# Scores of all twelve tiles from plain fp32 q and k, each product in a quarter of TensorE's array

## The chip, the core and the metric

The kernel runs on one core of a Trainium2 chip. The metric is device time in microseconds for one execution of the whole program. Below, PE is TensorE's matmul side and PEld its weight loads, DVE is VectorE, ACT ScalarE, POOL GpSimd and SP SyncE, which mostly issues DMAs.

## The reference

A gated linear attention (an mLSTM with a stabilised exponential gate) over 2 batches, 8 heads, 768 steps and a head size of 40; its output goes through a mixture of four dense experts and then through a gated product layer.

```python
for t in range(S):
    kt, vt, qt = (k[:, :, t], v[:, :, t], q[:, :, t])
    m_new = np.maximum(f_gate[:, :, t] + m, i_gate[:, :, t])
    ...
    C = f_stab[...] * C + i_stab[...] * np.einsum('bhd,bhe->bhde', vt, kt)
    n = f_stab[:, :, None] * n + i_stab[:, :, None] * kt
    h_tilde = np.einsum('bhde,bhe->bhd', C, qt)
    denom = np.maximum(np.abs(np.einsum('bhd,bhd->bh', n, qt)[:, :, None]), 1.0)
    y[:, :, t] = sigmoid(o_gate[:, :, t]) * h_tilde / denom
...
for e in range(E):                      # four experts, F = 1024, D = 320
    out += p[:, e:e + 1] * (np.maximum(x @ w1[e], 0.0) @ w2[e])
...
return ((x @ w_a) * (x @ w_b)) @ w_out  # d_ff = 1536
```

All inputs and the output are fp32.

## The kernel before

The 768 steps of each batch are cut into six chunks of 128, which gives twelve tiles; tile n is chunk n // 2 of batch n % 2. Within a tile the recurrence is solved in parallel form: the scores q k^T of each head (a 128 by 128 matrix, keys down the partitions) are multiplied by a matrix of gate weights and applied to v, and what older chunks contribute comes from a running state. A tile passes through these helpers, each one a few instructions:

- `load_qk` (L329) brings q and k, transposed, head dimension on the partitions, four heads side by side, once for each half hh of the heads;
- `w_exp` (L504 on ACT) and `w_mask` (L508 on POOL) make the gate weights `w_t`;
- the scores land in two PSUM banks `pt_c`, one for each half, and `s1b` (L530 on DVE) multiplies them into `w_t`;
- `s2a` (L541) applies them to v (`pt_y`, fp32, two column halves of the array side by side) and reads the state (`pt_i`, L547); `s2b`, `s2x` (L564) and `s2c` normalise, gate and pad the result `x_t`;
- `s3a` transposes it on PE (`pt_x`, L154 to L156), and `x_hi`, `x_lo` split it into two fp32r parts `xh`, `xl`, the input of the experts;
- `weigh_k`, `state` (`pt_u`, L604), `state_in`, `state_old`, `state_add` carry the state on.

The scores are made in two ways. Tiles 0 to 3 (n < NP = 4) use `scores2` (L510 to L518): q and k stay fp32, the two halves of the heads lie at partitions 0 and 64, and a product takes 40 rows of one half of the array's rows and all 128 columns; the heads are taken from the two halves in turn. Tiles 4 to 11 use `scores` (L520 to L526): q and k are loaded three times over into 120 rows, ACT casts all of it to fp32r (`split_qk`, L351), DVE or POOL replace one of three row groups of each operand by the rounding error (`low_qk`, L357), and one fp32r product over 120 rows then gives the score of a head in one pass.

Beside the tiles, from 17 us on, PE runs the first expert's products (`psa` L210, `psy` L289 to L291) as a stream of items; ACT and DVE evict each item (`hh` L277, `hl` L278), and ACT, POOL and DVE split the weights that come in (`wh` L78, `wl` L102). The place of every helper in this stream is written out by hand in the table `ev` (L711 to L809): pairs of a time, counted in items, and a helper; an engine's queue holds the instructions in that order. PSUM tiles of the helpers come from one pool of four banks (`ps_t`). At 151 us the tiles are through; the other experts and the last layer follow, in which PE is fed from SBUF alone.

Of the kernel before, what the change touches and what calls it, by code (L numbers as in the profile page):

```python
# [7 lines left out]
F32 = mybir.dt.float32  # L8
# [25 lines left out]
NP = 4  # L34
# [4 lines left out]
QB = 3  # L39
# [12 lines left out]
def mlstm_moe_kernel(ctx, tc, gates, qk, qc, kvo, dp, w1b, w2b, ident_d, bdmask_d, rsel_d, exp_d, out):  # L52
# [256 lines left out]
    with ExitStack() as c1:  # L309
# [19 lines left out]
        def load_qk(n, hh, eng=None):  # L329

            t = td.setdefault(n, {})
            if n < NP:
                if "two" not in t:
                    tag, bufs = ("qs", 2) if n == NP - 1 else ("qk", QB)
                    t["two"] = qp.tile([KS, 2, 512], F32, tag=tag, name="qk_t", bufs=bufs)
                at, r, to = 64 * hh, RQ, t["two"]
            else:
                to = t["qk", hh] = qp.tile([KS, 2, 512], F32, tag="qk", name="qk_t", bufs=QB)
                at, r = 0, KS
            v = to.rearrange("p a b -> p (a b)")  # L340
# [169 lines left out]
        def scores2(n):  # L510
# [3 lines left out]
            for h in range(4):  # L514
                hs = slice(h * P, (h + 1) * P)
                for hh in range(2):
                    v = t["two"][64 * hh:64 * hh + D]
                    nc.tensor.matmul(t["pc", hh][:, hs], v[:, 1, hs], v[:, 0, hs], start=True, stop=True, skip_group_check=True)  # L518

        def scores(n, hh, pool=ps_t, tag="t"):  # L520
            t = td[n]
            qs = t["qs", hh]
            t["pc", hh] = pc = pool.tile([P, 512], F32, tag=tag, name="pt_c")
            for h in range(4):
                hs = slice(h * P, (h + 1) * P)
                nc.tensor.matmul(pc[:, hs], qs[:, 1, hs], qs[:, 0, hs], start=True, stop=True, skip_group_check=True)  # L526
# [550 lines left out]
```

## Time and profile before

| | us |
|---|---|
| median of 3 runs | 597.9 (596.6 to 600.08) |
| the profiled execution | 597.87 |
| its span, first to last instruction | 596.1 |
| PE busy | 586.3, 98% of the span |
| PEld busy | 555.6, 93% |
| DVE busy | 395.2, 66% |
| ACT busy | 268.2, 45% |
| POOL busy | 190.5, 32% |

The profiled execution lies 0.03 us below the median. The 1.8 us between its time and its span lie around the program and are not touched by any instruction. A busy PE is one that has a matmul in flight, not one at its peak: matmuls are pipelined, a record lasts longer than the step to the next one, so what a product costs is read from the start of one to the start of the next.

### The profile page before, as it was taken

To read this page: it belongs to the slowest core of one execution; us is meant where nothing else is said; L and a number is where in the kernel's file an instruction comes from. 1 tells how busy PE (TensorE), PEld (TensorE's weight loads), DVE (VectorE), ACT (ScalarE), POOL (GpSimd) and SP (SyncE) were. 2 spreads that over 40 slices of the span, in tenths; PEclk is the share of its full clock that TensorE was granted. 3 is DMA by queue.
4 is the path that set the end of the run, shared out by engine and by line. 5 is a ranking of instruction groups with operands and counts; after the bars stand their busy time and mean duration, and the time that the engine had idled before them with its cause. 6 is when DMAs were issued, how large, how long until landed. Compare 5 with 4: busy or idle time off the path is not lost.

```text
span 596.1 us, 14965 instructions
## 1 busy us (share of the span) xinstructions
PE 586.3 (98%) x6108; PEld 555.6 (93%) x6108; DVE 395.2 (66%) x813; ACT 268.2 (45%) x606; POOL 190.5 (32%) x246
## 2 busy tenths in 40 slices
PE   8999999999999999999999999999999999999997
PEld 5798999999899999999999999999898989898887
DVE  6888877876423665645466666688688787875444
ACT  7879478683232444433233332334455534341211
POOL 3966665650010333544022231221323222311000
PEclk9999999999999999999999999999999999999999
DMA  8979648750211333332111211515312121200012
GB/s 238 272 227 241 177 135 231 186 154 1 60 40 54 80 86 107 92 89 52 36 40 38 57 40 39 143 53 153 115 42 73 39 58 52 63 21 2 1 38 97
DMA packets 34626, 55.48 MB, mean 93 GB/s; under 512 B 3861, under 2 KB 22461, under 8 KB 34557
## 3 DMA queue, kind: packets, MB, share of 16 engines
q10 hardware_dynamic: 18992, 27.07, 16.4%
q1 hardware_dynamic: 14893, 25.48, 15.9%
q0 software_dynamic: 672, 1.97, 1.2%
q8 instruction: 48, 0.79, 0.6%
q14 instruction: 21, 0.17, 0.1%
HBM read 50.15 MB, written 3.96 MB: 91 GB/s over the span
## 4 chain that ended last, share of the span: by engine, by line
PE 81%; DVE 7%; DMA 6%; ACT 2%; ACTq 2%; issue 2%; SPq 0%; DVEq 0%
PE psa L230 28%; PE psy L255 26%; PE psb L230 8%; PE psa L210 6%; DMA gt<-in_gates 3%; PE pt_y L541 2%; PE psy L289 2%; PE psy L291 2%; PE psy L290 2%; DMA qk_t<-in_qk 2%; PE pt_i L547 1%; PE pt_c L526 1%; PE pt_u L604 1%; DVE acc L300 1%; DVE g L914 1%
## 5 line engine op out<-in xcount | busy, mean ns | idle before, releaser
L255 PE MATMUL psy<-wh,hh 64*128 64x320 f32 x848 | 179.0, 306 | 1.5 <-ACT acc L890 1.5
L255 PE MATMUL psy<-wl,hh 64*128 64x320 f32 x848 | 178.7, 306 | 0.0
L255 PE MATMUL psy<-wh,hl 64*128 64x320 f32 x848 | 178.7, 306 | 0.0
L230 PE MATMUL psa<-xh,wh 64*128 64x512 f32 x648 | 147.5, 388 | 0.2 <-DVE g L914 0.2
L255 PEld LDWEIGHTS psy<-wh,hh 64*128 64x128 f32 x848 | 131.5, 184 | 2.6 <-ACT acc L890 1.9
L255 PEld LDWEIGHTS psy<-wh,hl 64*128 64x128 f32 x848 | 131.6, 184 | 0.0
L255 PEld LDWEIGHTS psy<-wl,hh 64*128 64x128 f32 x848 | 131.4, 184 | 0.0
L230 PE MATMUL psa<-xh,wl 64*128 64x512 f32 x468 | 109.4, 387 | 0.0
L230 PEld LDWEIGHTS psa<-xh,wh 64*128 64x128 f32 x648 | 92.9, 184 | 3.9 <-DVE g L914 0.8
L230 PE MATMUL psa<-xl,wh 64*128 64x512 f32 x432 | 95.3, 387 | 0.0
L911 DVE SCALAR_TENSOR_TENSOR hl<-psa,hh 128x512 fp32r<-128x512 f32 x72 | 46.3, 685 | 72.4 <-ACT hh L910 72.4
L134 POOL TENSOR_TENSOR wl<-tp,lf 128x272 fp32r<-128x272 f32 x48 | 39.1, 814 | 122.3 <-DVE tp L133 111.4
L230 PEld LDWEIGHTS psa<-xh,wl 64*128 64x128 f32 x468 | 69.6, 184 | 2.7
L230 PE MATMUL psb<-xh,wh 64*128 64x512 f32 x216 | 69.7, 388 | 0.0
L131 POOL TENSOR_TENSOR lf<-lf,sq 128x272 f32<-128x272 f32 x48 | 38.1, 795 | 95.4 <-ACT wh L130 72.2
L910 ACT ACTIVATE hh<-psa 128x512 fp32r<-128x512 f32 x72 | 39.1, 596 | 64.1 <-PE psy L255 33.4
L230 PEld LDWEIGHTS psa<-xl,wh 64*128 64x128 f32 x432 | 62.9, 184 | 2.5
L230 PE MATMUL psb<-xh,wl 64*128 64x512 f32 x180 | 58.2, 387 | 0.0
L130 ACT CAST wh<-tp 128x272 fp32r<-128x272 f32 x48 | 20.2, 420 | 68.7 <-DVE tp L127 66.4
L102 POOL TENSOR_TENSOR wl<-raw,wh 128x352 fp32r<-128x352 f32 (+1 forms) x30 | 28.4, 950 | 70.0 <-ACT wh L78 70.0
L230 PE MATMUL psb<-xl,wh 64*128 64x512 f32 x144 | 44.2, 387 | 0.0
L914 DVE TENSOR_TENSOR g<-psa,bs 128x512 f32<-128x512 f32 x36 | 24.7, 685 | 28.1 <-ACT bs L913 27.9
(147 smaller groups left out, 1254.5 us busy)
## 6 DMA issues: line engine op xcount, KB each, us to landing
raw<-in_w2b ACTq DMA_DIRECT2D x48, 272.0 KB, 2.8
qk_t<-in_qk SPq DMA_DIRECT2D x16, 480.0 KB, 6.2
raw<-in_w1b ACTq DMA_DIRECT2D x40, 176.0 KB, 2.3
acc<-in_w1b SPq DMA_DIRECT2D x22, 176.0 KB, 4.8
kvo_t<-in_kvo SPq DMA_DIRECT2D x10, 364.5 KB, 6.2
og_t<-in_kvo SPq DMA_DIRECT2D x6, 320.0 KB, 4.9
dz_t<-z_t ACTq DMA_DIRECT2D x12, 160.0 KB, 2.7
qc_t<-in_qc SPq DMA_DIRECT2D x10, 180.0 KB, 4.3
```

Of the source, the lines that this page charges most:

```text
L102: lo_eng.tensor_tensor(wl[:, ps], raw[:, k * st // parts:(k + 1) * st // parts], wh[:, ps].bitcast(F32), op=ALU.subtract)
L130: nc.scalar.copy(wh[:, cs], tf)
L131: nc.gpsimd.tensor_tensor(lf, lf, sq, op=ALU.mult)
L134: nc.gpsimd.tensor_tensor(wl[:, cs], tf, lf, op=ALU.add)
L210: nc.tensor.matmul(ps, l, r, start=(i == 0), stop=(i == len(prs) - 1))
L230: return nc.tensor.matmul(ps[g], w[rows, o:o + P], x, start=start, stop=stop)
L255: ms = [nc.tensor.matmul(ps[t], l[rows, t * P:(t + 1) * P], w[rows, off:off + DM], start=start, stop=stop) for t, rows in zip(two, (UP, DN))]
L289: nc.tensor.matmul(ps, lh, wh[:, off:off + DM], start=(fi == 0), stop=False)
L290: nc.tensor.matmul(ps, lh, wl[:, off:off + DM], start=False, stop=False)
L910: nc.scalar.activation(hh, ps[f], AF.Relu)
L911: nc.vector.scalar_tensor_tensor(hl, ps[f], 0.0, hh.bitcast(F32), op0=ALU.max, op1=ALU.subtract)
L914: nc.vector.tensor_tensor(g, ps[2 * f + 1], bs, op=ALU.mult)
```

## The change

`scores2` now serves all twelve tiles, and each of its products is cut in two along the keys: 40 rows of one half of the array by 64 of its 128 columns, so that a tile has sixteen products, each in a quarter of the array, where it had eight. `load_qk` loads 48 rows for each half of the heads for every tile (192 KB, where tiles 4 to 11 loaded 480 KB), into one of five buffers. `split_qk`, `low_qk` and `scores` are gone. `s2x` does all its steps in as many parts as it is told, which is two for tile 1 and one for all others; before, only its last product was cut. The table `ev` is written anew: besides the rows that fall away, many helpers stand at other places.

```diff
-NP = 4
...
-QB = 3
+QB = 5
...
         def load_qk(n, hh, eng=None):
 
             t = td.setdefault(n, {})
-            if n < NP:
-                if "two" not in t:
-                    tag, bufs = ("qs", 2) if n == NP - 1 else ("qk", QB)
-                    t["two"] = qp.tile([KS, 2, 512], F32, tag=tag, name="qk_t", bufs=bufs)
-                at, r, to = 64 * hh, RQ, t["two"]
-            else:
-                to = t["qk", hh] = qp.tile([KS, 2, 512], F32, tag="qk", name="qk_t", bufs=QB)
-                at, r = 0, KS
-            v = to.rearrange("p a b -> p (a b)")
-            (eng or nc.sync).dma_start(v[at:at + r], qk[n, hh, 0:r])
-
-        def split_qk(n, hh):
...
-            nc.scalar.copy(st, raw)
-            t["qs", hh] = st
-
-        def low_qk(n, hh, i, eng):
...
+            if "two" not in t:
+                t["two"] = qp.tile([KS, 2, 512], F32, tag="qk", name="qk_t", bufs=QB)
+            v = t["two"].rearrange("p a b -> p (a b)")
+            (eng or nc.sync).dma_start(v[64 * hh:64 * hh + RQ], qk[n, hh, 0:RQ])
...
                 for hh in range(2):
                     v = t["two"][64 * hh:64 * hh + D]
-                    nc.tensor.matmul(t["pc", hh][:, hs], v[:, 1, hs], v[:, 0, hs], start=True, stop=True, skip_group_check=True)
-
-        def scores(n, hh, pool=ps_t, tag="t"):
...
+                    for k in (UP, DN):
+                        nc.tensor.matmul(
+                            t["pc", hh][k, hs], v[:, 1, h * P + k.start:h * P + k.stop], v[:, 0, hs],
+                            start=True, stop=True, skip_group_check=True)
...
-            nc.vector.tensor_scalar(dn, y[:, :, D:DE], -1.0, 1.0, op0=ALU.mult, op1=ALU.max)
...
+            xu = a2.tile([P, H, D], F32, tag="y", name="xu_t", bufs=1) if j == 0 else xv
+            for p in range(parts):
+                hs = slice(p * H // parts, (p + 1) * H // parts)
+                nc.vector.tensor_scalar(dn[:, hs], y[:, hs, D:DE], -1.0, 1.0, op0=ALU.mult, op1=ALU.max)
+                nc.vector.tensor_tensor(dn[:, hs], y[:, hs, D:DE], dn[:, hs], op=ALU.max)
+                nc.vector.reciprocal(dn[:, hs], dn[:, hs])
+                nc.vector.tensor_tensor(xu[:, hs], y[:, hs, 0:D], dn[:, hs].to_broadcast([P, H // parts, D]), op=ALU.mult)
+                nc.vector.tensor_tensor(xv[:, hs], xu[:, hs], r[:, hs], op=ALU.mult)
...
-            (13.433, low_qk, 5, 0, 0, V), (13.8, w_exp, 5, 0), (14.14, gate_d, 3, V), (14.18, split_qk, 5, 1), (14.22, scores, 4, 1),
...
+            (11.68, w_mask, 4, 0), (11.76, scores2, 4), (11.84, s1b, 4, 0), (11.92, state_add, 3), (12.18, load_qk, 5, 1), (12.26, w_exp, 4, 1),
...
```

What the table does to the queues is shown at three places. The first is PE's queue around the scores of tile 4, the first tile that was split (`qs_t` holds the split q and k, `qk_t` the plain ones). Before, the second half of the heads of tile 4 and, behind the tile's product with v, the first half of tile 5:

```order
L210 MATMUL psa<-xh_75,wh_144 128x256
L210 MATMUL psa<-xh_75,wl_145 128x256
L526 MATMUL pt_c<-qs_t 128x128 x4
L541 MATMUL pt_y<-kvo_t,w_t 64x82 x8
L526 MATMUL pt_c<-qs_t 128x128 x4
L289 MATMUL psy<-wh_144,hh 128x320
L290 MATMUL psy<-wl_145,hh 128x320
```

After the change the scores of tile 4, lines being numbered anew (L496 is `scores2`, L209 and L288 to L290 are the expert's products):

```order
L288 MATMUL psy<-wh_393,hh 128x320
L289 MATMUL psy<-wl_394,hh 128x320
L290 MATMUL psy<-wh_393,hl 128x320
L496 MATMUL pt_c<-qk_t 64x128 x16
L209 MATMUL psa<-xh_75,wh_146 128x256
L209 MATMUL psa<-xh_75,wl_147 128x256
```

Eight products in two bursts of four, each of which read a freshly split `qs_t`, have become sixteen in one burst that reads what the DMA brought.

The second is ACT's queue from the second half of tile 4 to the end of tile 5 (L504, afterwards L481, is `w_exp`, which makes the gate weights `w_t`). Before:

```order
L504 ACTIVATE w_t_933<-Rr0_110,ET_889 128x128 x4
L277 ACTIVATE hh_950<-psa_952 128x256
L351 CAST qs_t_965<-qk_t_869 120x1024
L504 ACTIVATE w_t_977<-Rr1_111,ET_889 128x128 x4
L277 ACTIVATE hh_982<-psa_984 128x256
L351 CAST qs_t_996<-qk_t_931 120x1024
L504 ACTIVATE w_t_1023<-Rr1_111,ET_889 128x128 x4
```

After:

```order
L481 ACTIVATE w_t_974<-Rr0_110,ET_918 128x128 x4
L276 ACTIVATE hh_991<-psa_993 128x256
L481 ACTIVATE w_t_1012<-Rr1_111,ET_918 128x128 x4
L276 ACTIVATE hh_1017<-psa_1019 128x256
L276 ACTIVATE hh_1073<-psa_1075 128x256
L481 ACTIVATE w_t_1088<-Rr1_111,ET_918 128x128 x4
```

The casts are gone from between the evictions `hh`, and nothing has taken their place.

The third is DVE's queue just after the first two tiles, when the gates of the second chunk (`fa`, `df`, `lf`, `L`, `cm`) meet the evictions `hl` of the first items. Before:

```order
L393 SCALAR_TENSOR_TENSOR fa_387<-gt_177,fa_180 112x128
L397 TENSOR_TENSOR df_388<-fa_387,gt_177 112x128
L278 SCALAR_TENSOR_TENSOR hl_395<-psa_396,hh_394 128x256
L401 TENSOR_SCALAR lf_390<-df_388 112x128
L403 SCALAR_TENSOR_TENSOR L_408<-rmask_107,lf_390 112x128
L409 SCALAR_TENSOR_TENSOR cm_389<-df_388,L_408 48x128
L278 SCALAR_TENSOR_TENSOR hl_414<-psa_415,hh_413 128x256
```

After:

```order
L370 SCALAR_TENSOR_TENSOR fa_415<-gt_177,fa_180 112x128
L277 SCALAR_TENSOR_TENSOR hl_422<-psa_423,hh_421 128x256
L374 TENSOR_TENSOR df_416<-fa_415,gt_177 112x128
L277 SCALAR_TENSOR_TENSOR hl_437<-psa_438,hh_436 128x256
L378 TENSOR_SCALAR lf_418<-df_416 112x128
L380 SCALAR_TENSOR_TENSOR L_452<-rmask_107,lf_418 112x128
L386 SCALAR_TENSOR_TENSOR cm_417<-df_416,L_452 48x128
```

The first eviction moves ahead of `df`, the second ahead of `lf`, `L` and `cm`; both still stand behind `fa`, which reads the second chunk's gates.

## Rows read from the trace of the kernel before

**Rows 1.** Windows: busy us (count) of PE, PEld, DVE, ACT, POOL; clock, DMA share, GB/s.

```profile
0.00:17.00 17.00, 14.42 (x139) 9.53 (x139) 11.16 (x31) 12.05 (x25) 6.87 (x20) 1.00 0.90 250
17.00:20.00 3.00, 2.56 (x18) 2.05 (x16) 1.91 (x5) 2.38 (x8) 3.00 (x7) 1.00 1.02 301
20.00:30.00 10.00, 9.24 (x63) 8.46 (x64) 9.10 (x19) 8.55 (x24) 9.77 (x15) 1.00 1.05 250
...
45.00:60.00 15.00, 13.91 (x118) 13.29 (x117) 12.56 (x26) 13.50 (x35) 10.41 (x12) 1.00 0.94 242
```

**Rows 2.** Waits of PE from 17 to 151 us: total, times, longest.

```profile
PE psa L210 <- DVE hl L278: 1.0, 1, 1.0
PE pt_c L526 <- DVE qs_t L357: 0.7, 1, 0.7
PE pt_c L526 <- ACT qs_t L351: 0.4, 1, 0.4
```

**Rows 3.** Tile `pt_c`, its instructions: duration ns min/median/max, first and last start us.

```profile
L518 PE MATMUL pt_c<-qk_t x64: 272/272/373, 6.4 to 34.4; 40*128 40x128 f32 x64
```

**Rows 4.** Timeline of PE, scores of tile 3: start us, us, operation, [idle before].

```profile
32.71 0.85 PE L604 MATMUL pt_u<-kvo_t,kw_t 128*120 128x123 f32 x6
33.50 1.16 PE L518 MATMUL pt_c<-qk_t 40*128 40x128 f32 x16
34.59 0.38 PE L210 MATMUL psa<-xh,wh 128*128 128x256 f32 x1
34.81 0.28 PE L210 MATMUL psa<-xh,wl 128*128 128x256 f32 x1
34.93 0.28 PE L210 MATMUL psa<-xh,wh 128*128 128x256 f32 x1
```

**Rows 5.** The same, a window at the start of that burst.

```profile
33.50 0.38 PE L518 MATMUL pt_c<-qk_t 40*128 40x128 f32 x2
```

**Rows 6.** Timeline of PE, scores of tile 4, first half, and what follows.

```profile
49.80 0.66 PE L526 MATMUL pt_c<-qs_t 120*128 120x128 f32 x4
50.30 0.36 PE L289 MATMUL psy<-wh,hh 128*128 128x320 f32 x1
50.51 0.31 PE L290 MATMUL psy<-wl,hh 128*128 128x320 f32 x1
50.66 0.31 PE L291 MATMUL psy<-wh,hl 128*128 128x320 f32 x1
```

**Rows 7.** Timeline of PE around 57 us: rest of tile 4, start of tile 5.

```profile
56.92 0.63 PE L526 MATMUL pt_c<-qs_t 120*128 120x128 f32 x4 [0.67 <-DVE qs_t L357]
...
58.70 0.63 PE L526 MATMUL pt_c<-qs_t 120*128 120x128 f32 x4 [0.43 <-ACT qs_t L351]
```

**Rows 8.** Groups by line and shape: busy us, mean ns, idle before and its releasers.

```profile
L357 POOL TENSOR_TENSOR qs_t<-qk_t,qs_t 40x512 fp32r<-40x512 f32 x14 | 18.7, 1337 | 4.6 <-ACT qs_t L351 3.0 <-POOL w_t L508 0.9
L351 ACT CAST qs_t<-qk_t 120x1024 fp32r<-120x1024 f32 x16 | 16.7, 1046 | 3.6 <-DMA qk_t<-in_qk 3.1 <-PE pt_c L526 0.4
L357 DVE TENSOR_TENSOR qs_t<-qk_t,qs_t 40x512 fp32r<-40x512 f32 x18 | 16.6, 930 | 1.7 <-ACT qs_t L351 1.5
```

**Rows 9.** Timeline of DVE: end of tile 1, then the second chunk's gates.

```profile
14.42 0.20 DVE L572 RECIPROCAL dn_t<-dn_t 128x8 f32<-128x8 f32 x1
14.66 0.49 DVE L577 TENSOR_TENSOR xu_t<-pt_y,dn_t 128x320 f32<-128x320 f32 x1
15.18 0.74 DVE L580 TENSOR_TENSOR x_t<-xu_t,og_t 128x160 f32<-128x160 f32 x2
...
18.83 0.80 DVE L393 TENSOR_TENSOR_SCAN fa<-gt,fa 112x128 f32<-112x128 f32 x1 [0.80 <-DMA gt<-in_gates]
...
20.15 0.42 DVE L278 SCALAR_TENSOR_TENSOR hl<-psa,hh 128x256 fp32r<-128x256 f32 x1
```

**Rows 10.** Timeline of PE: a product with v, one half of a tile's heads.

```profile
31.77 0.79 PE L541 MATMUL pt_y<-kvo_t,w_t 128*64 128x82 f32 x16
32.49 0.30 PE L460 MATMUL pt_e<-ident,ex 96*128 96x96 f32 x1
```

More of the change, by code (lines that the diff above doesn't have):

```diff
@@ L761, in mlstm_moe_kernel @@
-            (14.733, load_o, 3, nc.sync), (14.867, gate4, 3), (15.136, weigh_k, 5), (15.173, low_qk, 5, 1, 0, nc.gpsimd),
-            (15.209, low_qk, 5, 1, 1, nc.gpsimd), (15.245, gate_c, 3), (15.282, s2a, 4, 1), (15.318, s2b, 4), (15.355, load_qk, 6, 0),
-            (15.391, load_kvo, 6), (15.427, gate5, 3), (15.464, send_L, 3, nc.sync), (15.644, s2x, 4), (15.689, s1b, 5, 0),
-            (15.733, table, AF.Sigmoid), (15.778, state_old, 4), (15.822, scores, 5, 1), (15.867, weigh_k, 4), (15.911, w_mask, 5, 1),
@@ L769, in mlstm_moe_kernel @@
-            (18.778, state_add, 5), (18.822, spread_L, 7, nc.scalar), (18.867, gate_tail, 3), (18.911, s2x, 5), (18.956, s2c, 5, P_),
-            (19.2, load_qk, 7, 0), (19.3, table, AF.Exp), (19.4, gate1, 4), (19.733, load_qk, 7, 1), (19.867, load_kvo, 7), (20.3, gate_out, 3),
-            (20.7, w_exp, 6, 0), (20.8, low_qk, 6, 1, 1, V), (20.9, low_qk, 6, 1, 0, nc.gpsimd), (21.18, split_qk, 7, 0), (21.26, s3a, 5),
-            (21.34, scores, 6, 0), (21.42, low_qk, 7, 0, 1, V), (21.733, gate_d, 4, nc.gpsimd), (21.867, w_mask, 6, 0),
@@ L801, in mlstm_moe_kernel @@
-            (39.3, split_qk, 11, 1), (39.34, scores, 10, 1), (39.38, low_qk, 11, 1, 1, V), (39.42, s1b, 10, 1), (39.46, split_qk, 11, 0),
-            (40.7, w_exp, 11, 0), (40.8, weigh_k, 10), (40.9, shift_x, 1), (41.7, low_qk, 11, 0, 1, nc.gpsimd), (41.8, low_qk, 11, 1, 0, V),
-            (41.9, low_qk, 11, 0, 0, V), (42.3, s2a, 10, 0), (42.64, s2a, 10, 1), (42.68, w_exp, 11, 1), (42.72, w_mask, 11, 0),
-            (42.76, scores, 11, 0), (42.8, s2b, 10), (42.84, w_mask, 11, 1), (42.88, s2x, 10), (42.92, scores, 11, 1), (42.96, s2c, 10, P_),
@@ L805, in mlstm_moe_kernel @@
[L805 to L808 removed]
+            (-39.1, load_v, 0), (-39, load_v, 1), (-38.9, load_o, 0, nc.sync), (-38.8, go, w0[0:1]), (-38.7, fill_R, 0), (-38.6, go, w0[3:4]),
@@ new lines, in mlstm_moe_kernel @@
+            (7.636, table, AF.Exp), (7.673, s2b, 2), (7.709, spread_L, 5, nc.sync), (7.745, s2x, 2), (7.782, load_qk, 4, 1),
+            (7.818, spread_L, 4, nc.sync), (7.855, s2a, 3, 0), (7.891, go, w2[2:3]), (7.927, s1b, 3, 1), (7.964, weigh_k, 2), (8.125, state, 1),
+            (8.15, s2c, 2, nc.scalar), (8.175, state_old, 1), (8.2, load_kvo, 4), (8.225, go, w2[3:4]), (8.25, state_in, 1), (8.275, s3a, 2),
+            (8.3, go, w2[3:4]), (8.325, go, w2[4:5]), (8.35, go, w2[4:5]), (8.375, state_add, 1), (8.4, x_hi, 2), (8.425, x_lo, 2),
@@ new lines, in mlstm_moe_kernel @@
+            (25.25, weigh_k, 6), (25.3, load_kvo, 8), (25.35, state, 6), (25.4, w_mask, 7, 0), (25.45, state_in, 6), (25.65, s1b, 7, 0),
+            (25.7, s2c, 6, nc.scalar), (25.75, load_qk, 8, 0), (25.8, w_mask, 7, 1), (25.85, s3a, 6), (25.9, spread_L, 8, nc.gpsimd),
+            (25.95, x_hi, 6), (26.233, state_add, 6), (26.367, gate4, 4), (26.625, s1b, 7, 1), (26.65, gate5, 4), (26.675, x_lo, 6),
+            (26.7, s2a, 7, 0), (26.725, s2a, 7, 1), (26.75, gate_tail, 4), (26.775, s2b, 7), (26.8, s2x, 7), (26.825, table, AF.Sigmoid),
@@ L809, in mlstm_moe_kernel @@
+            (45.92, s2c, 11, P_), (46.18, s3a, 11), (46.26, x_hi, 11), (46.34, x_lo, 11), (46.42, shift_x, 2),
         ]
```

178 lines of the change are left out of this document (71 added, 107 removed).

## The prediction

> **What bounds the kernel now.** I read the busy time by stage first, since the whole change lies in the first 151 us. From 20 to 30 us PE is idle 0.76 us of 10, from 45 to 60 us 1.09 of 15, and there ACT at 13.5 and DVE at 12.6 of 15 are nearly as full [rows 1]. So the stage is paced by PE: a microsecond of PE's queue is a microsecond of the time, and ACT, DVE, POOL and the DMAs count only where PE waits for them. Next the waits of PE in that stretch: three that the profile shows as idle, 2.1 us in all, of which two, 0.7 and 0.4 us, wait for the split of q and k [rows 2]. Then the scores themselves [rows 3 to 7], and the start, where the order of the work changes most [rows 9].
>
> **What a tile's scores cost on PE now.** A split tile runs as two bursts of four. One starts at 49.80 and the next operation at 50.30, thus 0.50 us; the operation after that comes 0.21 us later where the usual step of that kind is 0.15 [rows 6]. So about 2 x 0.55 = 1.1 us. A plain tile before the change, eight products in two halves of the rows, runs from 33.50 to 34.59, 1.09 us, and has wider edges: 0.22 us instead of 0.12 to the second operation behind it, and ahead, six records of the state product take 0.79 us until the scores start, though a record of that length should let its successor in after some 0.115 us (an estimate from the 0.12 between records of 0.28), 0.69 in all, so 0.1 us is lost [rows 4]. That is 1.29 us.
>
> **What the new form costs.** The operands give a product's 128 columns of q as the moving side in both forms, so cutting the keys in two does not shorten a product; it makes sixteen of eight. Whether that costs anything hangs on how many stand in the array together. There are 64 records for the 32 products of the four plain tiles [rows 3], so a product is two passes. The first two records of a burst fit into 0.38 us though one of them takes 0.373 [rows 3, 5], so two start together; and the steps say the same: 1.09 / 16 = 0.068 us a record, where the state product over the whole array steps by 0.79 / 6 = 0.13 with nearly the same width [rows 4]. The two halves of the rows do run side by side. So do the column halves of the product with v: 0.72 / 16 = 0.045 us a record of 82 columns [rows 10], against 0.13 x 82 / 123 = 0.087. No row shows both cuts at once. From below, four quarters run side by side: sixteen products in the time of eight, 1.09 us, and 1.24 with the edges when I take 0.05 us off because the first weights have half the columns (an estimate). From above, only two of the sixteen run together: 2 x 1.09 = 2.18 us. I take the lower end, since both cuts are shown to work singly and the four quarters share no cells. Against 1.1 us that is +0.15 to +0.2 us for each of tiles 4 to 11, **+1.5 us**. Tile 3 keeps its cost; tiles 0 to 2 lie in the start, below.
>
> The two passes that start within 0.01 us of each other lie in different halves of the rows [rows 3, 5], and they are one pass each of two products, since both passes of one product need the same cells. The Trainium skill has a rule against this (TensorE: Matmul & The Clock Gate, section "Part 3: Packing small matmuls — row/col tiling"): matmuls start and end strictly in the order of the program. By it, with the two passes of a product next to each other in the queue, a quarter would overlap with one neighbour alone, and the sum would be that of rival (a), 608.1. The pairs in this trace do not agree with it, as far as passes go.
>
> **What goes away.** Sixteen casts on ACT, 16.7 us, eighteen subtractions on DVE, 16.6 us, and fourteen on POOL, 18.7 us [rows 8]. All of it runs beside PE, so by itself it is worth nothing; it is worth the waits that it causes, 0.67 us for `low_qk` and 0.43 us for `split_qk` [rows 7]: **-1.1 us**. Behind them nothing else is late: the new scores read what the DMA brought, and 16 loads carry 48 rows of 4 KB instead of 120, at a place where the DMA share is 0.94 [rows 1]. What hides the 17 us or so of each engine is PE's own queue; were it shorter, they would count.
>
> **What is moved.** In the start, tile 1's `s2x` now runs in two parts: three small steps again, at 0.20 each or less 0.5 to 0.6 us, and the second step in two pieces, which by its neighbour costs 0.74 instead of 0.49 us [rows 9]: x of tile 1 is whole some 0.8 us later. The first item needs it. But PE then waits 1.0 us for the third item's eviction `hl`, which stands on DVE behind `df` and `fa`, and `fa` waits for the second chunk's gates until 18.83 [rows 2, 9]. So the later start is covered by that wait, whose end does not depend on tile 1. The new queue puts `hl` ahead of `df`, worth 0.46 us at most, while a cast that moved ahead of the eviction `hh` on ACT gives part of that back. On SP 320 KB for the first output gate go ahead of the first weights, 1.3 us of transfer at 250 GB/s [rows 1], but what is queued ahead of the second gates' load stays the same set, so `fa` starts as before. I count the start as **0**, from -1 (the waits at 17 to 30 us, 1.2 us of idle PE, mostly gone [rows 1]) to +0.8 (the later x not covered). The remaining moves in the table fill queues that have slack; a new wait of PE would be of the size of those there are, 0.4 to 1.0 us [rows 2], and I put none into the sum. Both score banks of a tile are now taken at once out of four, which is where one would arise.
>
> **The sum.** 597.87 + 1.5 - 1.1 + 0 = **598.3 us**. The profiled execution lies 0.03 us under the median of 597.9, so the sum stands for the median too. A measurement of this kernel can tell about 0.5%, 3 us, from no change: faster is below 594.9, slower above 600.9.
>
> **Rivals.**
> (a) Slower: the quarters run two at a time, because the second pass of a quarter holds up the first pass of the next one in PE's queue. Place: each of the twelve bursts. Price: 2.18 - 1.09 = 1.09 us for each of the nine tiles from 3 to 11, +9.8 us, **608.1 us**; it decides as soon as fewer than four stand together, by half as much where it is three. For it: four together need PE to look past six passes where two together need it to look past one or two, and no row shows four. Against: each pair of rows 4 and 5 already passes one that is held up. Chance 0.15.
> (b) Slower by less: four fit, but 32 records in a burst come faster than PE takes them. The densest rows now are sixteen in 0.72 us, 0.045 us each [rows 10]; 32 of these are 1.44 us, 0.35 more than 1.09, for nine tiles +3.2 us: **601.5 us**. For it: nothing in the trace is denser. Against: those sixteen may have been paced by their 82 columns. Chance 0.10.
> (c) Faster: the relief of ACT, DVE and POOL removes every wait of PE between 17 and 60 us, 0.44 + 0.76 + 1.09 = 2.3 us of idle [rows 1], the start ends 1 us earlier, and the edges of the bursts cost nothing, so that the scores come to about +0: 597.87 - 2.3 - 1 = **594.6 us**. For it: DVE and ACT at 13 of 15 us just where PE waits. Against: it needs all of it together, and PE's queue hardly waits after 60 us. Chance 0.15.
> (d) The change does nothing that shows: 1.5 and 1.1 us cancel, or both are smaller. That is inside the forecast.
>
> **How the numbers follow.** The forecast has 0.60, the rivals 0.15, 0.10 and 0.15. Faster: (c), 0.15. Same: the forecast, 0.60. Slower: (a) and (b), 0.25. The likeliest case alone runs from 596 (start -1, waits -1.1, scores 0) to 600.9 (start +0.8, one new wait of 1.0, nothing gained at the split). The range for 8 in 10 takes in (c) and (b), with room for (b) and a new wait together: 594.3 to 603.0; it leaves out (a) and a little more.
>
> **What would show it.** Right: `pt_c` with 32 records in each burst, the next operation 1.1 us after the first, and four records starting within some hundredths of a microsecond; PE's waits for `qs_t` gone; ACT and DVE some 16 us lower, with the time the same. Wrong: a burst of 2.2 us (a) or 1.4 us (b); PE idle by more than 2 us at a place where it was not; the first item of the experts later than 17.7 us and the third later than 20.6 us. Wrong in the other sense: the tiles through at 148 us instead of 151.

## The result, and the profile after

The change takes 601.39 us (median of 11 runs, 599.62 to 603.92) against 597.9: a ratio of 1.0064, with a 95% interval from 1.0050 to 1.0078. That is slower by 3.5 us; the forecast was 598.3, slower by 0.4. The time lies inside the range of 594.3 to 603.0, but beyond the likeliest case, which ended at 600.9, and beyond the 0.5% that divide no change from slower; slower had a chance of 0.25. The profiled execution is the shortest of the eleven, 599.62 us with a span of 597.9; against the 597.87 of the one before, it shows half of the loss.

The page's first line, after the change:

```profile
PE 587.7 (98%) x6363; PEld 554.9 (93%) x6364; DVE 378.5 (63%) x796; ACT 254.7 (43%) x591; POOL 169.9 (28%) x234
```

DVE is down by 16.7 us, ACT by 13.5, POOL by 20.6, and the span is 1.8 us longer: what was taken off these engines lay beside PE, as foreseen. PE's waits from 17 to 151 us, after:

```profile
PE pt_a L472 <- DVE Rr L456: 1.2, 1, 1.2
PE pt_x L153 <- DVE x_t L551: 0.8, 1, 0.8
PE psa L209 <- DVE xl L144: 0.3, 1, 0.3
```

The two waits for the split [rows 2] are gone, and `hl` as well; a wait of 1.2 us for `Rr`, the rows of the decay that DVE builds for the gate weights, is new. The windows of [rows 1], after (busy us and count of PE, PEld, DVE, ACT, POOL; clock, DMA share, GB/s):

```profile
0.00:17.00 17.00, 12.85 (x178) 8.15 (x179) 11.36 (x33) 11.19 (x21) 5.97 (x18) 1.00 0.91 245
17.00:20.00 3.00, 2.63 (x17) 2.00 (x19) 1.88 (x5) 2.58 (x8) 3.00 (x7) 1.00 1.01 297
20.00:30.00 10.00, 8.82 (x64) 8.14 (x63) 9.21 (x19) 8.96 (x24) 9.69 (x15) 1.00 1.05 279
45.00:60.00 15.00, 15.00 (x177) 14.22 (x175) 10.30 (x25) 8.99 (x28) 9.34 (x14) 1.00 0.77 198
```

From 45 to 60 us PE is now full (13.91 before), but up to 17 us it has lost 1.57 us and from 20 to 30 another 0.42.

Where the time goes can be summed between two marks of PE, the first product of the experts and the first of the stage behind the tiles (L230 before, L229 now). Before, the timeline has the second mark here:

```profile
151.41 0.50 PE L230 MATMUL psa<-xh,wh 64*128 64x512 f32 x2
```

and the window between the two marks reads:

```profile
16.95:151.41 134.46, 131.99 (x1228) 125.72 (x1226) 106.65 (x235) 92.67 (x227) 80.27 (x103) 1.00 0.66 176
```

The same two views, after:

```profile
153.67 0.50 PE L229 MATMUL psa<-xh,wh 64*128 64x512 f32 x2
```

```profile
18.20:153.67 135.47, 133.83 (x1435) 125.41 (x1433) 90.29 (x215) 79.22 (x212) 58.85 (x90) 1.00 0.50 138
```

The stage behind the tiles starts 2.26 us later. Of that 1.25 is the later first product, 1.84 more busy time of PE (133.83 - 131.99), and -0.83 less idle time (1.64 instead of 2.47).

Where in between it arises is seen at a product that stands behind the same work in both. The 89th product into `psy` starts at 65.72 us before and at 65.88 after, and by then PE has done the same products in both kernels, the scores of tiles 0 to 5 among them. Before, split there:

```profile
16.95:65.72 48.77, 46.39 (x411) 42.91 (x410) 41.89 (x91) 37.17 (x93) 37.26 (x53) 1.00 0.87 227
65.72:151.41 85.69, 85.59 (x819) 82.81 (x817) 64.77 (x145) 55.50 (x135) 43.01 (x50) 1.00 0.55 147
```

After:

```profile
18.20:65.88 47.68, 46.10 (x475) 42.61 (x474) 37.02 (x83) 32.78 (x89) 33.92 (x52) 1.00 0.73 197
65.88:153.67 87.79, 87.73 (x962) 82.80 (x960) 53.27 (x133) 46.44 (x124) 24.94 (x39) 1.00 0.37 105
```

The first product of the experts is 1.25 us late, but by the 89th into `psy` 1.09 of that is made up again, and 0.16 is left. The other 2.10 us come behind it, in tiles 6 to 11, where PE is idle for 0.1 us or less in either kernel.

Behind the second mark the profiles differ by one wait of PE alone, for ACT at about 430 us. It is 1.5 us before and 1.1 after, and between 0.4 and 1.7 us in the profiles of the kernels below; one profile of each does not tell whether its length belongs to the kernel or to the run, so it is left out of the argument. Before, and after:

```profile
PE psy L255 <- ACT acc L890: 1.5, 1, 1.5
```

```profile
PE psy L254 <- ACT acc L845: 1.1, 1, 1.1
```

**The burst.** The scores of tile 4 after the change, the timeline of PE from 52 to 53.8 us, and then the narrow window at the start of the burst:

```profile
52.08 0.31 PE L290 MATMUL psy<-wh,hl 128*128 128x320 f32 x1
52.32 1.12 PE L496 MATMUL pt_c<-qk_t 40*64 40x128 f32 x32
53.37 0.38 PE L209 MATMUL psa<-xh,wh 128*128 128x256 f32 x1
53.60 0.28 PE L209 MATMUL psa<-xh,wl 128*128 128x256 f32 x1
```

```profile
52.32 0.36 PE L496 MATMUL pt_c<-qk_t 40*64 40x128 f32 x4
```

All 32 records fit between 52.32 and 53.37, 1.05 us, and four of them start by 52.36: the four quarters do run together. With 0.09 lost ahead (0.24 instead of 0.15 to the start of the burst) and 0.11 behind it (0.23 instead of 0.12), a tile costs 1.25 us; 1.24 was forecast.

**The clock.** Each run also gives its mean granted clock. The two runs of the change with 1.000 take 599.62 and 599.74 us; the nine others, at 0.991 to 0.997, 600.53 to 603.92, with a median of 602.20. Where the clock fell in these nine is not shown. In the profiles of five experiments (e1 to e5) it fell in the start, in that of a sixth (e8) at 436.6 us.

### The profile page after: what moved, and what is told of

It reads as the page before. It is cut to its first block, busy times and chain, and to the rows that moved or that the text cites. A ratio compares the mean times of both kernels' runs of the same rounds, so it can differ in the third digit from the quotient of the medians.

```text
span 597.9 us, 15406 instructions
## 1 busy us (share of the span) xinstructions
PE 587.7 (98%) x6363; PEld 554.9 (93%) x6364; DVE 378.5 (63%) x796; ACT 254.7 (43%) x591; POOL 169.9 (28%) x234
## 3 DMA queue, kind: packets, MB, share of 16 engines
q10 hardware_dynamic: 18992, 27.07, 15.9%
## 4 chain that ended last, share of the span: by engine, by line
PE 84%; DVE 7%; ACT 3%; DMA 2%; ACTq 1%; issue 1%; DVEq 0%
PE psa L229 28%; PE psy L254 26%; PE psb L229 8%; PE psa L209 7%; PE psy L288 2%; PE pt_y L513 2%; PE psy L290 2%; PE psy L289 2%; PE pt_c L496 2%; PE pt_i L519 1%; DMA raw<-in_w2b 1%; PE pt_u L572 1%; DMA qk_t<-in_qk 1%; DVE g L869 1%; ACTq L821 1%
## 5 line engine op out<-in xcount | busy, mean ns | idle before, releaser
L254 PE MATMUL psy<-wh,hh 64*128 64x320 f32 x848 | 182.9, 306 | 1.1 <-ACT acc L845 1.1
L254 PE MATMUL psy<-wl,hh 64*128 64x320 f32 x848 | 182.7, 306 | 0.0
L254 PE MATMUL psy<-wh,hl 64*128 64x320 f32 x848 | 182.6, 306 | 0.0
L229 PE MATMUL psa<-xh,wh 64*128 64x512 f32 x648 | 148.6, 388 | 0.2 <-DVE g L869 0.2
L254 PEld LDWEIGHTS psy<-wh,hh 64*128 64x128 f32 x848 | 135.5, 184 | 2.2 <-ACT acc L845 1.5
L254 PEld LDWEIGHTS psy<-wh,hl 64*128 64x128 f32 x848 | 135.6, 184 | 0.0
L254 PEld LDWEIGHTS psy<-wl,hh 64*128 64x128 f32 x848 | 135.3, 184 | 0.0
L229 PE MATMUL psa<-xh,wl 64*128 64x512 f32 x468 | 110.2, 387 | 0.0
L229 PEld LDWEIGHTS psa<-xh,wh 64*128 64x128 f32 x648 | 94.6, 184 | 3.8 <-DVE g L869 0.8
L229 PE MATMUL psa<-xl,wh 64*128 64x512 f32 x432 | 96.3, 387 | 0.0
L229 PEld LDWEIGHTS psa<-xh,wl 64*128 64x128 f32 x468 | 70.5, 184 | 2.7
L229 PE MATMUL psb<-xh,wh 64*128 64x512 f32 x216 | 69.7, 388 | 0.0
L229 PEld LDWEIGHTS psa<-xl,wh 64*128 64x128 f32 x432 | 63.8, 184 | 2.6
L229 PE MATMUL psb<-xh,wl 64*128 64x512 f32 x180 | 58.2, 387 | 0.0
L129 ACT CAST wh<-tp 128x272 fp32r<-128x272 f32 x48 | 20.2, 421 | 67.2 <-DVE tp L126 65.3
L229 PE MATMUL psb<-xl,wh 64*128 64x512 f32 x144 | 44.2, 387 | 0.0
```

What stands on the lines that cost most here:

```text
L129: nc.scalar.copy(wh[:, cs], tf)
L229: return nc.tensor.matmul(ps[g], w[rows, o:o + P], x, start=start, stop=stop)
L254: ms = [nc.tensor.matmul(ps[t], l[rows, t * P:(t + 1) * P], w[rows, off:off + DM], start=start, stop=stop) for t, rows in zip(two, (UP, DN))]
```

## The experiments

The kernel before ran beside each of the three groups of kernels below. Its medians and the runs at a granted clock of 0.999 or more (count and median) go with the kernels of its group. Such runs are called runs at equal clock, or runs that kept the clock, below: in the three profiles with a mean of 0.999 (e7, f1, f2) the clock is under 1.00 only from 594.7 us on or later, where no matmul is left.

| kernel | runs | median us | ratio (95%) | at clock 0.999 or more: runs, median |
|---|---|---|---|---|
| the change | 11 | 601.39 | 1.0064 (1.0050 to 1.0078) | 2, 599.68 |
| before, with e1 to e4 | 21 | 598.02 | | 12, 597.38 |
| e1 old `s2x` | 10 | 601.74 | 1.0058 (1.0040 to 1.0076) | 3, 599.67 |
| e2 old start | 6 | 602.34 | 1.0077 (1.0048 to 1.0106) | 0 |
| e3 halves | 12 | 599.98 | 1.0042 (1.0025 to 1.0058) | 6, 599.73 |
| e4 loads | 6 | 601.94 | 1.0068 (1.0047 to 1.0089) | 1, 600.98 |
| before, with e5 to e8 | 27 | 598.25 | | 17, 597.73 |
| e5 before, quarters in tiles 0 to 3 | 12 | 597.65 | 0.9997 (0.9975 to 1.0019) | 5, 597.07 |
| e6 old start, halves | 11 | 599.43 | 1.0018 (1.0004 to 1.0031) | 8, 599.29 |
| e7 more warm-up | 10 | 601.15 | 1.0044 (1.0025 to 1.0063) | 5, 600.06 |
| e8 two at a time | 6 | 605.58 | 1.0129 (1.0105 to 1.0154) | 5, 605.64 |
| before, with f1 to f4 | 35 | 598.71 | | 19, 598.04 |
| f1 before, six plain tiles | 12 | 597.11 | 0.9975 (0.9963 to 0.9988) | 10, 596.90 |
| f2 before, less warm-up | 12 | 597.42 | 0.9981 (0.9964 to 0.9999) | 6, 597.37 |
| f3 old start, halves in tiles 0 to 2 | 12 | 600.45 | 1.0038 (1.0018 to 1.0058) | 8, 599.74 |
| f4 gates in the old order | 12 | 600.49 | 1.0029 (1.0016 to 1.0043) | 9, 600.40 |

**e1, the old `s2x`.** The profile of the change has x of tile 1 late, on DVE and then on PE:

```profile
14.96 0.70 DVE L551 TENSOR_TENSOR x_t<-xu_t,og_t 128x160 f32<-128x160 f32 x1
...
16.53 0.32 DVE L551 TENSOR_TENSOR x_t<-xu_t,og_t 128x160 f32<-128x160 f32 x1
```

```profile
14.74 1.09 PE L496 MATMUL pt_c<-qk_t 40*64 40x128 f32 x28 [1.23 <-DMA qk_t<-in_qk]
15.77 0.39 PE L616 MATMUL pt_w<-acc 128*128 128x512 bf16 x1
16.95 0.30 PE L153 MATMUL pt_x<-ident,x_t 128*128 128x128 f32 x1 [0.80 <-DVE x_t L551]
...
18.20 0.38 PE L209 MATMUL psa<-xh,wh 128*128 128x256 f32 x1
```

x is whole at 16.85 us (15.92 before, [rows 9]), so the small steps in two parts were the first suspect.

```diff
-            for p in range(parts):
-                nc.vector.tensor_scalar(dn[:, hs], y[:, hs, D:DE], ...)
+            nc.vector.tensor_scalar(dn, y[:, :, D:DE], ...)
```

> The change, with the old form of s2x (the three small steps and the product with the reciprocal once per tile, only the last product of tile 1 in two parts). Theory S (the loss is in the start): x of tile 1 is whole 0.8 us earlier than 16.85 us, the first item of the experts starts at 17.3 to 17.5 us instead of 18.20, and a run whose granted clock is 1.0 takes 598.8 to 599.1 us instead of 599.6 to 599.7. Theory Q (the loss is the quarters of the scores): the start comes earlier but the time stays within 0.3 us of the change, 599.4 to 599.9 at clock 1.0, since a later wait of VectorE takes the gain. On the clock: the change showed mean granted clocks of 0.991 to 1.0, with 0.8 to 4.2 us more wherever the clock was lower. If the gap of PE ahead of the transposes (15.8 to 16.95 us, filled by one warm-up product) brings the clock down, all runs here are at 1.0, median 599; if the gap ahead of tile 2's scores (13.5 to 14.74 us) does, most runs stay under 1.0 and the median is 600.5.

Both theories miss something. At equal clock nothing is gained: 599.67 (three runs) against 599.68 (two), where theory S had 598.8 to 599.1. In its profile, one with a fallen clock, the transposes waited for the identity matrix from DMA instead, until 18.28 us, so x was not what set the first item there.

**e2, the old start.** All rows of the table up to time 4.0 come from the kernel before, with the old `s2x`.

> The change, with the old s2x and all rows of the table up to time 4.0 as in the kernel before (the same set of helpers in the old order), so that only tiles 3 to 11 and the quarters differ from the kernel before. Theory S: first item at 16.9 to 17.1 us, no wait of PE on q and k over 0.7 us, the granted clock 1.0 in every run, and the time 597.2 to 598.2 us, since scores at about +0.1 to +0.15 us a tile and waits at -1.0 us nearly cancel. Theory Q: first item as early, but the time 599 us or more, because the scores of tiles 4 to 11 take it.

The expectation failed, and in a telling way: but for the quarters the start is the old one, and yet no run of six kept the clock. The windows of its profile, the clock being the number behind the counts:

```profile
13.00:17.00 4.00, 1.54 (x33) 1.10 (x33) 2.34 (x8) 2.52 (x7) 1.62 (x4) 0.98 1.05 319
17.00:20.00 3.00, 2.84 (x11) 2.17 (x12) 1.34 (x4) 2.15 (x7) 3.00 (x7) 0.50 1.01 297
20.00:24.00 4.00, 4.00 (x31) 3.79 (x30) 3.36 (x9) 2.99 (x6) 4.00 (x8) 0.97 1.01 296
```

PE is busy for 1.54 of the 4 us ahead of 17 us, and from 16.8 us on the granted clock is 0.50, the lower level of 1.2 GHz, until 20.2 us. The transposes and the first item run there at half speed.

**e3, halves.** Eight products of 128 columns for all tiles.

```diff
-                    for k in (UP, DN):
-                        nc.tensor.matmul(t["pc", hh][k, hs], v[:, 1, h * P + k.start:h * P + k.stop], v[:, 0, hs], ...)
+                    nc.tensor.matmul(t["pc", hh][:, hs], v[:, 1, hs], v[:, 0, hs], ...)
```

> The change, with the scores of all twelve tiles as eight products in halves of the rows (128 columns of k each) instead of sixteen in quarters. Theory S: a burst of a tile is 1.05 to 1.1 us in both forms, so at the same granted clock the time stays within 0.5 us of the change (599.2 to 600.1 at clock 1.0), first item at 18.2 us as in the change. Theory Q: the quarters lose at least 0.15 us a tile against the halves, so this is faster by 1.5 us or more: 598.1 or less at clock 1.0.

At equal clock it takes 599.73 (six runs) against 599.68 (two): no cost of the quarters against the halves is seen, as theory S had it. A burst of halves, in its profile:

```profile
59.12 1.16 PE L495 MATMUL pt_c<-qk_t 40*128 40x128 f32 x16
60.21 0.41 PE L288 MATMUL psy<-wh,hh 128*128 128x320 f32 x1
```

1.09 us to the next operation, 0.04 more than in quarters. What does differ is the clock: six of twelve runs kept it, two of eleven with quarters.

**e4, two loads moved back.**

```diff
-(-38.9, load_o, 0, nc.sync), ... (-37.9, load_qk, 2, 1),
+(-38.07, load_o, 0, nc.sync), (-38.05, load_qk, 2, 1),
```

> The change, with two issues on SP's queue moved back: the second half of tile 2's q and k goes ahead of the fifth piece of the first weights, and the 320 KB of the first output gate stand behind tile 2's first half instead of ahead of all weights. Theory S: PE's wait of 1.2 us ahead of tile 2's scores is gone or under 0.6 us; the first item stays at 18.1 to 18.3 us, since x of tile 1 sets it, and a run at clock 1.0 stays at 599.4 to 599.9 us. If that gap brings the clock down in the change, every run here is at 1.0 and the median falls from 601.4 to 599.7; if the gap ahead of the transposes does, most runs stay under 1.0, median 601. Theory Q gives no difference in either.

The wait for tile 2's loads was still 0.9 us in its profile and a second one of 1.1 us stood ahead of the transposes; the clock fell in five of six runs. Putting two loads back did not bring the clock back, and since the gap was not removed either, this run does not tell the two gaps apart.

**e5, quarters in the kernel before.** Only `scores2`, tiles 0 to 3, with the edit of e3 turned round.

> The kernel before, with one thing of the change alone: the plain scores of tiles 0 to 3 in quarters. Of 21 runs of the kernel before, 9 had a mean granted clock of 1.000 and 12 one of 0.994 to 0.999, and those were about 1.4 us longer at 0.997. Theory K (the quarters themselves let the clock fall in the start, where three of their bursts stand among gaps of PE): most runs fall under 0.998, mean clock 0.9955 to 0.9970, median 599 to 600.5 us. Theory G (gaps and late loads of the new order do it, not the form of the products): clocks and time as in the kernel before, median 597.5 to 598.3 us, since a burst in quarters takes 0.05 us less than one in halves.

Between the theories: 5 of 12 runs kept the clock, where 17 of 27 of the kernel before did, a difference that chance can make; the time is the same. In its profile the clock fell, the first item comes 2.83 us later than before and the stage behind the tiles 2.10.

**e6, old start and halves.** e2 with the edit of e3.

> The second experiment (old start, old s2x) with halves of the rows instead of quarters in all twelve tiles, so that the start is that of the kernel before, product for product, and only tiles 4 to 11 are new: plain instead of split. Theory K: the clock is 1.0 or 0.999 in about as many runs as in the kernel before, median 597.0 to 598.3 us against 602.3 with quarters. Theory G, in the form that the later part of the change makes the loads of the start later: clocks of 0.994 to 0.997 in all runs again, median 601 to 602.5 us.

The clock came back, 8 of 11 runs, as theory K had it. Its windows, against those of e2:

```profile
13.00:17.00 4.00, 3.20 (x30) 2.13 (x26) 3.04 (x10) 3.49 (x10) 2.04 (x5) 1.00 1.08 342
17.00:20.00 3.00, 2.62 (x18) 2.11 (x16) 1.90 (x5) 2.36 (x8) 3.00 (x7) 1.00 0.95 281
20.00:24.00 4.00, 3.31 (x25) 3.31 (x26) 3.77 (x10) 3.57 (x9) 4.00 (x8) 1.00 1.00 286
```

But the median of 599.43 is over the 597.0 to 598.3 expected: with the old start, the old products in it and the clock kept, 1.6 us are still lost (599.29 against 597.73). What is new in this kernel are tiles 4 to 11 and the rows that moved with them; from the 89th product into `psy` to the stage behind the tiles its profile takes 88.13 us, where the kernel before takes 85.69.

**e7, more warm-up.**

```diff
+(-31.95, warm_up, 5),
-(-31.5, warm_up, 1),
+(-31.5, warm_up, 5),
```

> The change, with nine more warm-up products on PE in the start: five ahead of tile 2's scores and four more ahead of the transposes, in the two stretches in which PE waits anyway (13.5 to 14.7 and 16.2 to 16.95 us). They compute nothing that is used. If gaps of PE let the clock fall, it is now 1.0 in nearly all runs and the median comes down from 601.4 to 599.2 to 600.0 us, where the two undisturbed runs of the change stand. If the narrow products of the scores do it whatever stands around them, the clocks stay at 0.991 to 0.997 in most runs and the median at 601 to 602.5 us.

Half of the runs kept the clock, so neither answer is right. The warm-up fills the gaps in part, and tile 2's loads came 1.3 us later in the profiled execution than in that of the change. Inconclusive.

**e8, two quarters at a time.** The sixteen products of a tile in another order.

```diff
-            for h in range(4):
-                for hh in range(2):
-                    for k in (UP, DN):
+            for k in (UP, DN):
+                for h in range(4):
+                    for hh in range(2):
```

> The change, with the sixteen quarter products of a tile in another order: all for the first half of the keys, then all for the second, so that neighbours in PE's queue fill two quarters at most. It is rival (a) of the prediction made on purpose. If quarters of different columns overlap only when they stand next to each other in the queue, a burst lasts 1.6 to 1.8 us from its first record to its last instead of 0.84, and the time at equal clock rises by 9 x 0.85 = 7.7 us for tiles 3 to 11 and up to 2.5 for tiles 0 to 2: 607 to 610 us. If PE sorts them out whatever their order, burst and time are as in the change.

Slower, but by 6.0 us at equal clock (605.64 against 599.68) and not by 7.7 or more. A burst in its profile, and the records that touch each of three stretches of it:

```profile
52.79 1.62 PE L496 MATMUL pt_c<-qk_t 40*64 40x128 f32 x32
54.34 0.39 PE L209 MATMUL psa<-xh,wh 128*128 128x256 f32 x1
```

```profile
53.05:53.31 0.26, 0.26 (x9) 1.00 0.78 219
53.31:53.58 0.27, 0.27 (x14) 1.00 1.09 260
53.58:53.84 0.26, 0.26 (x16) 1.00 0.94 251
```

1.55 us to the next operation instead of 1.05; twelve times 0.5 are 6.0. The records do not name their half of the keys, but their starts tell them apart: pairs follow each other every 0.109 us from the beginning, and at 53.32, when ten records have started, a second row of pairs sets in beside the first. Read so, the products of the second half start beside the last six records of the first, and PE takes up records that stand some way behind others that have to wait.

This profile has a mean clock of 0.997, and its fall lies far from the start, behind a wait of PE for ACT of 1.5 us:

```profile
436.00:440.00 4.00, 4.00 (x33) 3.89 (x34) 1.32 (x3) 3.24 (x9) 0.00 (x0) 0.57 0.22 68
```

So a mean clock under 0.999 does not by itself say that the start lost it.

**f1, plain scores for tiles 4 and 5 only.** The kernel before with `NP = 6`, tiles 3 to 5 in quarters, tiles 0 to 2 in halves; the rows of the table for the split of tiles 4 and 5 are dropped.

```diff
-NP = 4
+NP = 6
-(11.425, scores, 4, 0),
+(11.425, scores2, 4),
-(14.42, scores, 5, 0),
+(14.42, scores2, 5),
```

> The kernel before with plain scores for tiles 4 and 5 too, the two whose split PE waits for; tiles 6 to 11 stay split. Tiles 3 to 5 are in quarters, tiles 0 to 2 in halves as they were. Theory W (a plain tile costs PE 0.2 us more than a split one, and what speaks for it is only the waits for the split, 1.1 us, at 56.9 and 58.7 us): PE's idle time from 45 to 60 us falls from 1.1 us to under 0.2, and the time by 1.1 - 2 x 0.2 = 0.7 us against the kernel before, 597.2 to 597.8 against a median of 598.2. Rival: PE waits for something else in the same place (the mask or the weights of tile 5), idle stays over 0.7 us and the time within 0.3 us of the kernel before.

Theory W holds in the main, and this is faster than both kernels: 597.11 us, 0.9975 of the kernel before (0.9963 to 0.9988); at equal clock -1.1 us, where 0.7 had been expected. From 45 to 60 us, its window and its only wait:

```profile
45.00:60.00 15.00, 14.74 (x167) 13.98 (x169) 9.95 (x24) 9.86 (x32) 8.51 (x12) 1.00 0.94 233
```

```profile
PE pt_c L519 <- ACT dec L470: 0.3, 1, 0.3
```

PE is idle for 0.26 us there, a little more than the 0.2 expected. The gain is not seen whole in this profile, one of its longest runs: up to the 89th product into `psy` it is 0.68 us shorter than the kernel before, counted from the first item, as theory W has it, and from there to the stage behind the tiles 0.66 longer. What made the median faster than the theory stays open; PE's wait at about 430 us is 0.4 us here and 1.5 in the profile of the kernel before.

**f2, less warm-up in the kernel before.** The rows `warm_up, 1`, `warm_up, 1` and `warm_up, 2` of the start are dropped.

> The kernel before without the four warm-up products that stand on PE around the transposes of the start (14.8 and 16.4 us); they compute nothing that is used. Of 48 runs of the kernel before, 22 lay under a mean granted clock of 0.998. If the clock of the start hangs on how much PE has to do there, it now falls in most runs (0.991 to 0.997) and the median rises by 1 to 2 us, 599.2 to 600.2. If it hangs on something else, clocks and time stay, 597.8 to 598.5.

The clock was kept in 6 of 12 runs, 19 of 35 with them: no difference to be seen. The time is not higher but 0.2% lower, just distinguishable. Little hangs on these products. Of the 48 runs named in the expectation 19 lay under 0.998, not 22, and of the 21 named in that of e5 eight had a clock of 1.000, not nine.

**f3, old start with halves in tiles 0 to 2, quarters later.**

```diff
+                    for k in (slice(0, P),) if n < 3 else (UP, DN):
```

> The second experiment (old start, old s2x), with the quarters for tiles 3 to 11 alone and halves of the rows for tiles 0 to 2, so that up to 30 us PE has the products of the kernel before and every later tile those of the change. Theory K (quarters in the start let the clock fall): clocks of 1.0 or 0.999 in more than half of the runs, as with halves everywhere (11 runs, 8 of them so), and a median of 598.6 to 599.4 us, 0.0 to 0.5 under that with halves. Rival (the clock hangs on the rows after the start, or on chance in the loads): clocks of 0.994 to 0.997 in all runs and 601.5 to 602.5 us, as with quarters everywhere (6 runs).

The clock as theory K expects, kept in 8 of 12 runs; the same kernel with quarters in these three tiles (e2) kept it in none of 6. The median is 1 us over the upper end of the expectation; at equal clock it is 599.74, 1.7 us over the kernel before and no better than the change, although its first item comes at 16.82 us, as early as in the kernel before. Its profile, the shortest of its runs, has the stage behind the tiles at 152.45 us, 1.2 ahead of the change.

**f4, the gates on DVE in the old order.** The wait for `Rr`, in the change, on PE and on DVE:

```profile
26.93 0.48 PE L472 MATMUL pt_a<-Rr,LT 112*128 112x512 f32 x1
...
29.54 0.71 PE L472 MATMUL pt_a<-Rr,LT 112*128 112x512 f32 x2 [1.18 <-DVE Rr L456]
```

```profile
27.31 2.08 DVE L456 TENSOR_TENSOR Rr<-zx,rsel 64x512 fp32r<-64x512 f32 x2
29.32 0.41 DVE L277 SCALAR_TENSOR_TENSOR hl<-psa,hh 128x256 fp32r<-128x256 f32 x1
```

Two pieces of `Rr` stand on DVE from 27.31 to 29.4 us. The change has tile 3's first half ahead of tile 2's second, which PE wants first.

```diff
+(1.34, hi_L, 1, V), (1.35, low_L, 1),
-(2.18, hi_L, 1, V), (2.26, low_L, 1),
-(3.68, build_R, 3, V, 0, 4),
+(3.68, build_R, 2, V, 4, 8),
-(3.92, build_R, 2, V, 4, 8),
+(3.92, build_R, 3, V, 0, 4),
```

> The change, with VectorE's steps for the second chunk's gates in the old order (the cast of L ahead of that of cm, tile 2's second half of the rows of the decay ahead of tile 3's first), and halves for tiles 0 to 2 as in the third experiment of this batch. Theory S: PE's wait of 1.2 us for those rows at 28 to 29.5 us falls under 0.4 us, and a run at clock 1.0 takes 598.5 to 599.0 us instead of 599.7; with the clock of the third experiment (6 of 12 runs at 1.0) the median is 599.0 to 599.8. Rival: the wait only moves to another step of VectorE (an eviction hl), and at clock 1.0 it is 599.4 to 599.9 as in the change.

Theory S falls here. The wait is gone, and two others have come, PE's waits from 17 to 60 us in its profile:

```profile
PE psa L209 <- DVE hl L277: 0.9, 1, 0.9
PE pt_c L496 <- ACT dec L447: 0.8, 1, 0.8
```

At equal clock 600.40 (nine runs), no better than the change. This suggests, and no run shows it, that the chain of gate steps on DVE and ACT has about a microsecond too much to do between 20 and 35 us, and that the order only chooses where PE notices it.

## Why the prediction was right, and where it was wrong

The time fell into the range, but 3.1 us above the sum and 0.5 beyond the likeliest case. The range took it in because it had room for rival (b) and a new wait together, and (b) did not happen; that part of the hit is luck. The burst and the waits at the split came out as summed, the price of a plain tile against a split one was too small, the start was late where it had been counted as 0, and the clock had no term.

- **The quarters run four at a time**: right, and rival (a) is refuted in the trace (1.05 us a burst, not 2.18), as is (b) (not 1.44). The rule of the Trainium skill that was weighed there (TensorE: Matmul & The Clock Gate, section "Part 3: Packing small matmuls — row/col tiling"), start and end strictly in the order of the program, does not hold for passes here: four start within 0.04 us although each product has two. e8 shows that order counts all the same, but at 0.5 us a tile instead of the 1.09 that rival (a) was priced at; by the starts of its records PE looks past those that wait. The 0.05 us taken off for narrower weights rested on no row; the burst came out 0.04 to 0.06 us shorter than one in halves, for a reason that is not shown.
- **"Against 1.1 us that is +0.15 to +0.2 us for each of tiles 4 to 11, +1.5 us"**: right in kind, too small, and the largest miss. The plain tile came out at 1.25 as summed, but the split tile was set too high from tile 4 alone. Before, a later tile of the split kind reads:

```profile
113.90 0.56 PE L526 MATMUL pt_c<-qs_t 120*128 120x128 f32 x4
114.30 0.84 PE L604 MATMUL pt_u<-kvo_t,kw_t 128*120 128x123 f32 x6
114.90 0.64 PE L526 MATMUL pt_c<-qs_t 120*128 120x128 f32 x4
115.38 0.27 PE L460 MATMUL pt_e<-ident,ex 96*128 96x96 f32 x1
```

  0.40 and 0.48 us, where 0.50 had been taken twice. From the 89th product into `psy` to the second mark the six tiles from 6 on cost 2.10 us, 0.35 a tile, where 1.24 and 1.29 less 1.1 are 0.14 to 0.19 (1.5 is eight times the upper one). It is so whatever the start and the clock there: that stretch takes 87.78 to 87.80 us in all seven profiles with plain quarters four at a time (the change, e1, e2, e4, e7, f3, f4) and 88.13 in e3 and e6 with halves, against 85.68 to 85.75 in the kernel before, e5 and f2, where tiles 4 to 11 are split. The bursts explain about 0.27 of the 0.35 (1.25 less 0.88 and two edges of 0.05); the rest may lie in the rows that moved with them, which no run separates.
- **-1.1 us for the split waits**: right. From 45 to 60 us PE has 1.09 us less idle time. f1 takes this gain with two plain tiles instead of eight, and is 1.1 us faster than the kernel before at equal clock.
- **"I count the start as 0"**: this step failed. The first item came at 18.20 us, beyond the 17.7 that was to count against the forecast, and the third at 21.08, beyond the 20.6. As foreseen, the old wait for `hl` swallowed most of that: idle time of PE from the first item on fell by 0.89 up to 25 us. But then the wait for `Rr` adds 1.2 us, which the prediction had left out of the sum as "a new wait". In the two profiles the start so costs some 1.6 us and not 0. The 1.1 us gained at the split stand against it, and at the 89th product into `psy` the change is 0.16 us late, where the terms (0, -1.1 and two tiles at 0.19) have it 0.7 early. How much of this the new table of the start does is not shown. f1, with the old table, had its first item at 18.25 us in its profile, behind a wait of 1.5 us for q and k. And the whole old start (f3, e6) brought the first item back to 16.82 and 17.01 us, but the time at equal clock only to 599.74 and 599.29. e1 and f4 each took one cause away, and another wait took its place; e2 had no run at equal clock.
- **The granted clock** stood in no term. The profile of before reads 1.00 in all the windows shown, so it could not be seen there that the clock of this kernel falls in some runs, though 35 of its 83 runs, as given with the experiments, lie below 0.999. The median of the change lies 1.7 us above its two runs at full clock, that of the kernel before 0.5 to 0.7 above its own. By this estimate 1.0 to 1.2 of the 3.5 us are the clock, and 2.3 to 2.5 remain, near the 2.26 between the two marks of the profiles.

What sets the clock is told by the runs in part. With quarters four at a time in tiles 0 to 2 (the change, e1, e2, e4, e5) it was kept in 11 of 45 runs, and with nine more warm-up products (e7) in 5 of 10. With halves there (the kernel before, e3, e6, f1, f3, f4) it was in 89 of 142, and with four warm-up products less (f2) in 6 of 12. The sharpest pairs, equal but for this form, are e2 against f3 and e6, 0 of 6 against 8 of 12 and 8 of 11; they ran in different groups, but the kernel before kept it in 12 of 21, 17 of 27 and 19 of 35 in the three. The pair within one group, e5 against the kernel before, is 5 of 12 against 17 of 27 and decides nothing. In the five profiles where it fell in the start, PE had been idle for 1.5 to 2.5 of the 4 us from 13 to 17; but it was so for 2.0 in the profile of the change and for 1.5 in that of f1, where the clock held. Why the form counts, if it does, stays open: bursts of both forms take nearly the same time, and with quarters two at a time (e8) the clock was kept in 5 of 6 runs and fell outside the start in the sixth.

The rest of the ledger is not closed either. The six plain tiles from 6 on, f3 against f1 at equal clock, cost 2.8 us by the medians, and 1.45 by the traces, from the 89th product into `psy` to the stage behind the tiles; the profiled execution of f3 was its shortest, that of f1 among its longest.

The rivals: (c), faster because all waits vanish, was wrong, since new waits took their place; (d), nothing that shows, was wrong as well, since the interval lies clear of no change. What happened stands in none of them: a dearer plain tile, a later start and the clock, each about 1 us, all on the same side.

## What to carry to other kernels

Taking work off engines that wait for the bound one is worth the waits that it causes. Here these were two tiles' worth, and a change of these two tiles alone (f1) beats the change of all twelve, which pays some 0.35 us on PE for each of the six tiles that had no wait. Price a product from several of its places, not from the first. In a start in which several engines and the DMAs meet, ask what is late next when one wait goes, and do not count it as 0. To find where a loss arises, compare the two profiles at a product that stands behind the same work in both. And where runs of the same kernel show granted clocks below 1.0, look for the stretch in a profile that has one, since the mean does not say where it lies.

## What was not expected of the hardware

Records of PE pass others that wait, as the starts in e8 read: those of one column half start when six of the other half still stand ahead of them in the queue. Four fp32 products of 40 rows by 64 columns run in the array together at 0.109 us for a pass of each.

The granted clock fell to 0.50 in the start in the profiles of five kernels, e1 to e5, and stayed there from 16.8 to 20.2 us in e2 and from 17.0 to 23.8 in e1, most of it with PE fully busy. In all five it fell behind the end of PE's wait for the q and k of tile 2: in e3 the wait ends at 15.0 us and the clock falls at 15.3, in e1 at 15.9 and 17.0, in e2 at 14.5 and 16.8, by then in a second gap. f1 has the same wait, 1.5 us up to 15.2, and kept the clock. One such stretch is what the mean clocks of 0.993 to 0.997 stand for in these profiles, and in e8 one from 436.6 to 440.0 us. The runs of the kernel before with means below 0.999 are 1.3 to 1.6 us longer in each of the three groups.
